# Folded expert operands on their way through DRAM: a head's 128 rows in one run, a batch's tile gathered by four loads of 32 rows

## Chip, core and metric

One core of a Trainium2 chip runs the whole program. The metric is device time in microseconds for one execution, as the median of several runs. Beside it stands one profiled execution with its trace; all rows in this document come from such a trace.

## What is computed

Three stages follow each other: an attention through 32 packed queries per head, a mixture of four experts on all tokens, and a last two-layer network.

```python
def _attn_ref(q, k, v, p):              # q, k, v: (4, 8, 576, 64), p: (4, 8, 32, 64)
    p_packed = sm_attn(p, k, v)
    return sm_attn(q, p_packed, p_packed)

def _moe_ref(x, domain_probs, w1, w2):  # x: (2304, 512), w1: (4, 512, 1024), w2: (4, 1024, 512)
    p = domain_probs / (domain_probs.sum(-1, keepdims=True) + 1e-09)
    for e in range(E):
        h = np.maximum(x @ w1[e], 0.0)
        out += p[:, e:e + 1] * (h @ w2[e])

def _moe2_ref(x, w_in, w_out, s, b):    # w_in: (512, 2048), w_out: (2048, 512)
    r = np.maximum(x @ w_in, 0.0)
    return (s * (r * r) + b) @ w_out
```

The attention's second product ends in `p_packed` and `x @ w1[e]` begins with it, so the kernel folds the two: it multiplies `p_packed` of a batch into `w1[e]` once, and the expert's first layer then reads the attention's second softmax directly. The folded operand of one expert and one batch is 256 rows (8 heads of 32 packed queries) by 1024 columns, held as two float32r parts whose sum is the float32 value.

## The kernel before

**Steps of the expert stage.** `ua` lists 256 steps: 4 experts, 4 batches, 2 halves of 288 tokens, 8 blocks of 128 hidden columns. In step i the program first runs the side work entered for that step in the table `weave` (`run`), then the first layer `m1` (line 681, 6 matmuls) of step i + 2, then the second layer `m2` (line 709, 12 matmuls) of step i. One expert and batch is 16 steps. ScalarE and VectorE split each hidden tile into two parts (lines 691 and 692) between the two. All engines work through their instructions in order, so what ScalarE or VectorE waits for in side work delays the hidden tiles behind it, and with them TensorE.

**Folded operands of experts 2 and 3.** `fold_heads` (line 478, 6 matmuls) multiplies packed heads into one piece of `w1`: for expert e, column half n, group gi of four heads, head x of a pair and z, it makes 128 rows (4 batches of 32 rows) by 512 columns. ScalarE writes the first part (line 484), VectorE the second (line 485), both into a tile `w1o` of 512 KB. There are eight folds for an expert, two `w1o` tiles each. `store_heads` (line 493) writes each tile to `w1p_dram` two steps later in the program: 16 stores an expert, 32 in all, issued by SP. `load_w1p` (line 503) reads from there what one batch needs: a tile `w1p` of 128 partitions by 1024 numbers (512 KB) for each of n = 0, 1 and gi = 0, 1, so 4 tiles a batch and 32 in all. A row of such a tile is one piece of 4 KB in DRAM. For odd batches the two heads x are swapped, as the other operand is.

**Slots.** `w1o` tiles, raw pieces of `w1` (`load_w1b`, split at line 468) and raw pieces of the last network's weights (`last_weights`, lines 570 and 575) share seven slots `q0` to `q6` of SBUF. `take` hands out the slot given back longest ago; a `w1o` slot is given back when its store is issued, so the next writer of that slot waits until the store has read it.

**Places in the table.** For expert 2 the folds of n = 0 stand in steps 105, 107, 109 and 111, those of n = 1 in 114, 116, 118 and 120; for expert 3 in 153 to 159 and 178 to 184. A store stands two steps behind its fold. The loads of an expert's batch 0 stand in the batch before it, in steps 6, 7, 13 and 14 of its 16; those of batches 1 to 3 in steps 0, 1, 2, 3 of the batch before, 14 or more steps ahead of use. Between expert 1's and expert 2's last batch, and so between 2 and 3, SP also loads the eight pieces of `w2` (line 539), each three steps ahead of its split, and all through the expert stage the weights of the last network go through a conversion: a raw load, four free steps later the first VectorE work on it (line 582), and a store (line 605).

**SP's queue.** All of these transfers but a few of ScalarE's are issued by SP in program order, an instruction each. Eight semaphores (`DMAHW0` to `DMAHW7`) take turns, so an issue also waits for the transfer eight places before it.

Of the kernel before, what the change touches and what calls it, by code (L numbers as in the profile page):

```python
# [8 lines left out]
F32 = mybir.dt.float32  # L9
# [10 lines left out]
def attention_experts_mlp_kernel(  # L20
# [26 lines left out]
    B, H, S, D = q.shape  # L47
# [4 lines left out]
    P = 128  # L52
    G = 2
# [17 lines left out]
    dram = ctx.enter_context(tc.tile_pool(name="dram", bufs=1, space=DRAM))  # L71
# [9 lines left out]
    def f32(ap):  # L81
        return ap.bitcast(F32)
# [276 lines left out]
    def give(tag):  # L359
        free4.append(tag)  # L360
# [35 lines left out]
    def w1p_tile(e, bi, c):  # L396
# [8 lines left out]

    HF = F // 2
    w1p_dram = {
        e: dram.tile([2, B, 64, 2, G, 2 * HF], F32, name=f"w1p_dram{e}")
        for e in range(2, E)
    }  # L410

# [78 lines left out]
    def store_heads(e, n, gi, x):  # L490
        for z in range(2):
            q, t = w1o.pop((e, n, gi, x, z))
            nc.sync.dma_start(  # L493
                out=w1p_dram[e][x, :, 32 * z : 32 * z + 32, n, gi],
                in_=f32(t).rearrange("a x f -> a (x f)"),
            )
            give(q)

    def load_w1p(e, bi, n, gi):
        pool = wodd if bi % 2 else keep  # L500
        t = pool.tile([P, 2, HF], F32R, tag="w1p", bufs=4, name=f"w1p_{e}{bi}{n}{gi}")
        for half in range(2):
            nc.sync.dma_start(
                out=f32(t[64 * half : 64 * half + 64]).rearrange("a x f -> a (x f)"),
                in_=w1p_dram[e][half ^ bi % 2, bi // 2 * 2 + half, :, n, gi],
            )
        w1p[e, bi, n, gi] = t

# [380 lines left out]
    with tc.manual_schedule():  # L889
# [3 lines left out]
        for gi in range(G):  # L893
# [4 lines left out]
            out=dp.rearrange("a j e -> a (j e)"),  # L898
            in_=probs.rearrange("(a j) e -> a (j e)", a=P),
# [161 lines left out]
        for e in range(E):  # L1061
            for bi in range(B):
# [12 lines left out]
                for c in range(4):  # L1075
                    n, gi = divmod(c, 2)
                    if ne > 1:
                        d = c if nb else (6, 7, 13, 14)[c]
                        at(s0 + d, load_w1p, ne, nb, n, gi)
                    if bi != B - 1 or ne < 2:  # L1080
                        continue
                    for x in range(2):
                        k = 2 * c + x
                        if n:
                            d = s0 + 2 * k - 7
                        elif ne == 2:
                            d = s0 - SB + 8 + 2 * k
                        else:
                            d = s0 - 2 * SB + NF + 2 * k
                        if x == 0:  # L1090
                            at(d - 4, load_w1b, ne, n, gi)
                        at(d, split_w1b, ne, n, gi, x)
                        at(d + 1, fold_heads, ne, n, gi, x)
                        at(d + 3, store_heads, ne, n, gi, x)
# [158 lines left out]
```

## Time and profile before

| | |
|---|---|
| median of 3 runs | 1201.96 us (1201.61 to 1205.5) |
| profiled execution | 1199.96 us, of which the span of the trace is 1198.2 us |
| TensorE matmul busy | 1122.3 us (94%) |
| VectorE, ScalarE, GpSimd busy | 683.7, 397.5, 288.5 us |
| DMA | 175.06 MB, 146 GB/s on average |
| mean granted TensorE clock | 0.970 of full speed |

TensorE is busy nearly all the time, so what is to be read is where it is not, and where it runs at a lower clock. The DMA share is the mean busy share of the core's 16 DMA engines; divided into the GB/s of the same stretch it tells how fast a busy engine moves data.

### The profile page before, as it was taken

What the parts mean: (1) busy time and instruction counts of PE and PEld (TensorE: products, weight loads), DVE (VectorE), ACT (ScalarE), POOL (GpSimd) and SP (SyncE); (2) the same over time, 40 slices, a digit from 0 to 9 for tenths busy, and PEclk for the clock granted to TensorE, in tenths of its full rate; (3) what the DMA queues carried; (4) which work ended last, traced back from release to release, by engine and by line L of the source; (5) the groups of instructions that cost most, each with busy time, mean ns of one, the idle gap of its engine ahead of it and who ended that gap; (6) DMA issues with size and microseconds to landing.
All of it is one profiled execution on the core that took longest, in us unless ns stands there. A gap on an engine that the chain in (4) does not pass through costs nothing.

```text
span 1198.2 us, 18356 instructions
## 1 busy us (share of the span) xinstructions
PE 1122.3 (94%) x7147; PEld 1047.0 (87%) x7147; DVE 683.7 (57%) x1257; ACT 397.5 (33%) x780; POOL 288.5 (24%) x345
## 2 busy tenths in 40 slices
PE   7999999999997769997976999999999999999998
PEld 5889999999996669987866999998999999999996
DVE  7866664576562315643531664357984576576654
ACT  4422223543441213331322332234563242233221
POOL 1430202233321114311313434335420111011000
PEclk9999999999998889998897999999999999999999
DMA  8624220133043446636334664133675655655532
GB/s 258 163 88 110 59 74 26 36 107 112 31 140 129 148 147 162 193 119 201 123 132 152 176 178 125 51 149 139 243 291 192 210 190 198 218 184 195 185 132 79
DMA packets 67590, 175.06 MB, mean 146 GB/s; under 512 B 10032, under 2 KB 26672, under 8 KB 67504
## 3 DMA queue, kind: packets, MB, share of 16 engines
q1 hardware_dynamic: 66656, 172.79, 44.8%
q8 instruction: 56, 0.92, 0.3%
q10 hardware_dynamic: 848, 1.11, 0.3%
q14 instruction: 30, 0.25, 0.1%
HBM read 127.44 MB, written 46.44 MB: 145 GB/s over the span
## 4 chain that ended last, share of the span: by engine, by line
PE 76%; DMA 14%; DVE 5%; issue 1%; SPq 1%; POOL 1%; ACT 1%; DVEq 0%; POOLq 0%; ACTq 0%
PE acc L709 27%; PE o L867 16%; PE h L833 14%; PE h L681 14%; DMA w1p_dram<-w1o 6%; DMA w2r<-in_moe_w_dram 4%; DMA wi11raw<-in_moe_w_in_dram 1%; DMA w1p<-w1p_dram 1%; PE s L289 1%; PE pw L379 1%; SPq L493 1%; PE pp L522 1%; DVE kT L152 1%; PE s L181 1%; PE pv L235 1%
## 5 line engine op out<-in xcount | busy, mean ns | idle before, releaser
L709 PE MATMUL acc<-hh,w2l 128*128 128x288 f32 x1024 | 310.0, 303 | 11.5 <-DVE y L724 10.8
L709 PE MATMUL acc<-hh,w2h 128*128 128x288 f32 x1024 | 309.5, 302 | 0.0
L709 PE MATMUL acc<-hl,w2h 128*128 128x288 f32 x1024 | 309.3, 302 | 0.0
L681 PE MATMUL h<-a,w1p 128*128 128x288 f32 x1536 | 262.0, 308 | 36.2 <-DVE hl L692 34.1
L681 PEld LDWEIGHTS h<-a,w1p 128*128 128x128 f32 x1536 | 226.0, 195 | 50.0 <-DVE hl L692 36.1
L692 DVE SCALAR_TENSOR_TENSOR hl<-h,hh 128x288 fp32r<-128x288 f32 x256 | 116.0, 453 | 213.7 <-ACT hh L691 212.2
L867 PE MATMUL o<-wo,gg 128*128 128x512 f32 x864 | 223.7, 393 | 3.5 <-DVE gg L801 1.9
L709 PEld LDWEIGHTS acc<-hh,w2l 128*128 128x128 f32 x1024 | 199.4, 195 | 12.6 <-ACT w1h L468 6.6
L833 PE MATMUL h<-xs,wop 128*128 128x384 f32 x1008 | 204.3, 339 | 0.7 <-DVE y L724 0.7
L709 PEld LDWEIGHTS acc<-hh,w2h 128*128 128x128 f32 x1024 | 199.7, 195 | 0.0
L709 PEld LDWEIGHTS acc<-hl,w2h 128*128 128x128 f32 x1024 | 199.5, 195 | 0.0
L833 PEld LDWEIGHTS h<-xs,wop 128*128 128x128 f32 x1008 | 181.0, 189 | 13.8 <-DVE y L724 1.4
L867 PEld LDWEIGHTS o<-wo,gg 128*128 128x128 f32 x864 | 160.8, 188 | 27.7 <-DVE gg L801 2.3
L691 ACT ACTIVATE hh<-h 128x288 fp32r<-128x288 f32 x256 | 104.2, 408 | 215.0 <-PE h L681 214.0
L735 POOL TENSOR_TENSOR x<-x,y 128x288 f32<-128x288 f32 (+2 forms) x144 | 88.1, 648 | 206.2 <-DVE y L724 206.2
L853 DVE TENSOR_TENSOR yy<-h,uv 128x384 f32<-128x384 f32 x96 | 51.0, 551 | 47.6 <-PE h L833 47.5
L787 ACT ACTIVATE yy<-yy 128x768 f32<-128x768 f32 x48 | 40.3, 839 | 113.3 <-DVE yy L853 113.3
L485 DVE TENSOR_TENSOR w1o<-pp,w1o 128x512 fp32r<-128x512 f32 x32 | 21.4, 688 | 82.4 <-ACT w1o L484 82.4
L547 POOL TENSOR_TENSOR w2l<-w2r,w2h 128x512 fp32r<-128x512 f32 x32 | 41.5, 1307 | 111.2 <-ACT w2h L546 109.6
L797 ACT ACTIVATE gg<-yy,b_sb 128x768 fp32r<-128x768 f32 x48 | 44.8, 934 | 37.3 <-DVE yy L790 36.0
L801 DVE SCALAR_TENSOR_TENSOR gg<-yy,b_sb,gg 128x768 fp32r<-128x768 f32 x48 | 55.4, 1155 | 1.6 <-ACT gg L797 1.6
L790 DVE SCALAR_TENSOR_TENSOR yy<-yy,s_sb 128x768 f32<-128x768 f32 x48 | 51.2, 1066 | 0.0
(370 smaller groups left out, 1027.4 us busy)
## 6 DMA issues: line engine op xcount, KB each, us to landing
xs<-xs_dram SPq DMA_DIRECT2D x63, 768.0 KB, 4.8
w1p_dram<-w1o SPq DMA_DIRECT2D x32, 512.0 KB
w1p<-w1p_dram SPq DMA_DIRECT2D x64, 256.0 KB, 7.7
xs_dram<-xs SPq DMA_DIRECT2D x21, 768.0 KB, 3.8
w2r<-in_moe_w_dram SPq DMA_DIRECT2D x32, 256.0 KB, 8.5
w1r<-in_moe_w_dram SPq DMA_DIRECT2D x12, 512.0 KB, 6.9
pb<-pn_dram SPq DMA_DIRECT2D x16, 288.0 KB, 13.6
out_dram<-o_sb SPq DMA_DIRECT2D x17, 256.0 KB, 2.0
```

Source lines behind the costliest of these rows:

```text
L547: nc.gpsimd.tensor_tensor(out=lo, in0=raw, in1=f32(hi), op=ALU.subtract)
L681: nc.tensor.matmul(t[:, :HT], lhsT=w1p_block(e, bi, f, gi, w), rhs=a2[bi][:, x, gi, tok], start=(n == 0), stop=(n == 3 * G - 1),)
L691: nc.scalar.activation(xh, t[:, :HT], AF.Relu)
L692: nc.vector.scalar_tensor_tensor(out=xl, in0=t[:, :HT], scalar=0.0, in1=f32(xh), op0=ALU.max, op1=ALU.subtract)
L709: nc.tensor.matmul(acc[m][:, :HT], lhsT=w[:, col], rhs=x, start=(f == 0 and n == 0), stop=(f == NF - 1 and n == 2),)
L735: nc.gpsimd.tensor_tensor(out=dst, in0=dst, in1=y[:, a - t0 : z - t0], op=ALU.add)
L790: nc.vector.scalar_tensor_tensor(out=y, in0=y, scalar=s_sb, in1=y, op0=ALU.mult, op1=ALU.mult)
L797: nc.scalar.activation(t[:, 0], y, AF.Identity, bias=b_sb)
L801: nc.vector.scalar_tensor_tensor(out=t[:, 1], in0=y, scalar=b_sb, in1=f32(t[:, 0]), op0=ALU.add, op1=ALU.subtract)
L833: nc.tensor.matmul(ps, lhsT=w[:, a, col], rhs=x[:, z, m, :], start=(n == 0), stop=(n == 3 * HK - 1),)
L853: nc.vector.tensor_tensor(out=dst, in0=ps, in1=src, op=ALU.add)
L867: nc.tensor.matmul(o_acc[i], lhsT=lhsT, rhs=w, start=(f == 0 and n == 0), stop=(f == FG - 1 and n == 2),)
```

## The change

The DRAM buffer gets another order of its dimensions, and the loads follow. Before, it is indexed [x, batch, row of 64, n, gi, column], and the 64 rows of a batch hold head z = 0 and then z = 1. A store of 128 rows therefore goes to 4 runs of 32 rows, the runs 64 rows apart. After, it is indexed [x, z, row of 128, n, gi, column]: a store's 128 rows lie one behind the other (each still a piece of 4 KB, 16 KB from the next), and a tile is gathered by 4 loads of 32 rows in place of 2 loads of 64 rows. Bytes, matmuls and vector work are the same.

```diff
     w1p_dram = {
-        e: dram.tile([2, B, 64, 2, G, 2 * HF], F32, name=f"w1p_dram{e}")
+        e: dram.tile([2, 2, P, 2, G, 2 * HF], F32, name=f"w1p_dram{e}")
...
             nc.sync.dma_start(
-                out=w1p_dram[e][x, :, 32 * z : 32 * z + 32, n, gi],
+                out=w1p_dram[e][x, z, :, n, gi],
                 in_=f32(t).rearrange("a x f -> a (x f)"),
...
-        for half in range(2):
+        for p in range(4):
+            half, z = divmod(p, 2)
+            r = 32 * (bi // 2 * 2 + half)
             nc.sync.dma_start(
-                out=f32(t[64 * half : 64 * half + 64]).rearrange("a x f -> a (x f)"),
-                in_=w1p_dram[e][half ^ bi % 2, bi // 2 * 2 + half, :, n, gi],
+                out=f32(t[32 * p : 32 * p + 32]).rearrange("a x f -> a (x f)"),
+                in_=w1p_dram[e][half ^ bi % 2, z, r : r + 32, n, gi],
             )
```

SP's instructions in the second half of expert 2's folds: stores, the first tiles of batch 0, the first pieces of `w2` (`w2r`). In the names, `w1o_21000` is expert 2, n = 1, gi = 0, x = 0, z = 0; `w1p_2000` is expert 2, batch 0, n = 0, gi = 0. Before:

```order
L493 DMA w1p_dram2_88<-w1o_21000_4515 4x32x1024
L493 DMA w1p_dram2_88<-w1o_21001_4518 4x32x1024
L503 DMA w1p_2000_4635<-w1p_dram2_88 64x1024 x2
L493 DMA w1p_dram2_88<-w1o_21010_4579 4x32x1024
L493 DMA w1p_dram2_88<-w1o_21011_4582 4x32x1024
L539 DMA w2r_20_4654<-in_moe_w2_dram 128x512
L503 DMA w1p_2001_4679<-w1p_dram2_88 64x1024 x2
```

And after:

```order
L493 DMA w1p_dram2_88<-w1o_21000_4515 128x1024
L493 DMA w1p_dram2_88<-w1o_21001_4518 128x1024
L505 DMA w1p_2000_4635<-w1p_dram2_88 32x1024 x4
L493 DMA w1p_dram2_88<-w1o_21010_4579 128x1024
L493 DMA w1p_dram2_88<-w1o_21011_4582 128x1024
L541 DMA w2r_20_4656<-in_moe_w2_dram 128x512
L505 DMA w1p_2001_4681<-w1p_dram2_88 32x1024 x4
```

The order stays; a store is one run of 128 rows where it was 4 runs of 32, and each tile takes four issues where it took two.

SP's instructions where expert 2's last batch is fetched while expert 3's first stores go out, with a raw weight piece (`wi11raw`) among them. Before:

```order
L493 DMA w1p_dram3_89<-w1o_30101_5901 4x32x1024
L503 DMA w1p_2300_6003<-w1p_dram2_88 64x1024 x2
L503 DMA w1p_2301_6033<-w1p_dram2_88 64x1024 x2
L493 DMA w1p_dram3_89<-w1o_30110_5962 4x32x1024
L493 DMA w1p_dram3_89<-w1o_30111_5965 4x32x1024
L503 DMA w1p_2310_6066<-w1p_dram2_88 64x1024 x2
L605 DMA wi_dram4_94<-wi9a_6038 128x512
L570 DMA wi11raw_6072<-in_moe2_w_in_dram 128x4x256
L503 DMA w1p_2311_6097<-w1p_dram2_88 64x1024 x2
```

And after:

```order
L493 DMA w1p_dram3_89<-w1o_30101_5925 128x1024
L505 DMA w1p_2300_6027<-w1p_dram2_88 32x1024 x4
L505 DMA w1p_2301_6059<-w1p_dram2_88 32x1024 x4
L493 DMA w1p_dram3_89<-w1o_30110_5986 128x1024
L493 DMA w1p_dram3_89<-w1o_30111_5989 128x1024
L505 DMA w1p_2310_6094<-w1p_dram2_88 32x1024 x4
L607 DMA wi_dram4_94<-wi9a_6066 128x512
L572 DMA wi11raw_6102<-in_moe2_w_in_dram 128x4x256
L505 DMA w1p_2311_6127<-w1p_dram2_88 32x1024 x4
```

Six more issues stand ahead of `wi11raw` in this stretch; nothing else has moved.

## Rows read from the trace of the kernel before

**Rows 1.** The page, part 1: busy time, share of the span, instructions.

```profile
PE 1122.3 (94%) x7147; PEld 1047.0 (87%) x7147; DVE 683.7 (57%) x1257; ACT 397.5 (33%) x780; POOL 288.5 (24%) x345
```

**Rows 2.** Stretches, m1 (L681) alone: length, busy (xmatmuls), granted clock, DMA share, GB/s.

```profile
363.30:454.70 91.40, 23.09 (x108) 19.66 (x109) 0.81 0.40 142
529.80:550.80 21.00, 4.89 (x24) 4.29 (x25) 0.76 0.41 143
562.80:576.80 14.00, 2.77 (x12) 2.42 (x13) 0.76 0.31 107
613.60:659.30 45.70, 11.47 (x54) 9.85 (x55) 0.81 0.47 159
659.30:731.10 71.80, 28.72 (x180) 25.47 (x181) 1.00 0.59 161
596.00:613.60 17.60, 6.05 (x36) 5.01 (x37) 1.00 0.25 77
```

**Rows 3.** The same stretches, folds (L478) alone; no fold in the two left out.

```profile
363.30:454.70 91.40, 6.36 (x30) 2.83 (x30) 0.81 0.40 142
529.80:550.80 21.00, 1.24 (x6) 0.48 (x6) 0.76 0.41 143
...
613.60:659.30 45.70, 1.23 (x6) 0.48 (x6) 0.81 0.47 159
...
596.00:613.60 17.60, 2.91 (x18) 1.45 (x18) 1.00 0.25 77
```

**Rows 4.** The longest of these stretches, all engines: PE, PEld, DVE, ACT, POOL busy.

```profile
363.30:454.70 91.40, 63.05 (x356) 57.93 (x355) 22.05 (x46) 18.93 (x42) 17.10 (x24) 0.81 0.40 142
```

**Rows 5.** Who waited for whom, ScalarE, whole span: total us, times, longest.

```profile
ACT w1o L484 <- DMA w1p_dram<-w1o: 70.7, 15, 9.6
ACT w2h L546 <- DMA w2r<-in_moe_w_dram: 45.9, 8, 10.8
```

**Rows 6.** Chain of waits, 340 to 460 and 510 to 670: start us, us, what.

```profile
by line: DMA w1p_dram<-w1o 33.9%; DMA w2r<-in_moe_w_dram 25.9%; PE acc L709 12.0%; PE h L681 6.7%; SPq L493 5.5%; SPq L539 2.8%; SPq L503 2.8%; issue 2.7%; DVE w1o L485 1.7%; DVE hl L692 1.7%; PE pp L478 1.5%; ACT w1o L484 1.5%; ACT hh L691
356.98 20.17 DMA w1p_dram<-w1o
412.88 13.54 DMA w2r<-in_moe_w_dram
538.84 15.05 DMA w1p<-w1p_dram
553.90 15.52 DMA wi11raw<-in_moe_w_in_dram
```

**Rows 7.** Stretches ruled by one kind of transfer, all engines; last: clock, DMA share, GB/s.

```profile
379.50:384.00 4.50, 3.98 (x17) 4.01 (x18) 2.52 (x7) 0.00 (x0) 4.04 (x8) 0.50 0.25 101
526.00:534.00 8.00, 6.43 (x49) 5.63 (x47) 1.56 (x3) 2.09 (x5) 0.00 (x0) 1.00 0.27 108
700.50:704.00 3.50, 3.50 (x29) 3.50 (x28) 2.25 (x5) 1.28 (x3) 2.82 (x4) 1.00 1.03 235
864.70:866.70 2.00, 2.00 (x12) 1.80 (x11) 2.00 (x2) 0.00 (x0) 2.00 (x2) 1.00 0.95 393
102.00:104.00 2.00, 2.00 (x26) 1.66 (x22) 0.71 (x3) 0.00 (x0) 0.00 (x0) 1.00 0.91 240
```

**Rows 8.** Instructions of tiles and lines: ns min/median/max, first and last start; landing us.

```profile
L503 SPq DMA_DIRECT2D w1p<-w1p_dram x64: 444/587/4942, 395.7 to 738.2; - x64
L493 SPq DMA_DIRECT2D w1p_dram<-w1o x32: 503/563/4167, 351.8 to 632.2; - x32
L484 ACT ACTIVATE w1o<-pp x32: 592/597/600, 349.1 to 628.2; 128x512 fp32r<-128x512 f32 x32
L485 DVE TENSOR_TENSOR w1o<-pp,w1o x32: 679/691/693, 349.7 to 628.9; 128x512 fp32r<-128x512 f32 x32
wi_dram<-wi14a SPq DMA_DIRECT2D x1, 256.0 KB, 2.1
...
DMA to landing us min/median/max: 5.4/7.7/17.2
```

## The prediction

> **What bounds the kernel now.** I read the page first: TensorE's matmuls are busy for 94% of the span [rows 1], so only stretches where TensorE is not fed can give time back. The 40 slices of the page show them around 350 to 460, 530 to 580 and 610 to 660 us. Next I asked for the busy time of such stretches with m1 alone, because its matmuls count the steps of the expert stage: six are one step [rows 2]. The stretch from 659.3 to 731.1 has 180 matmuls, 30 steps, at full granted clock: 71.80 / 30 = 2.393 us a step, undisturbed. A fold adds its six matmuls [rows 3]: from 596.0 to 613.6 there are 6 steps and 3 folds, (17.60 - 6 x 2.393) / 3 = 1.08 us each. With these two prices every disturbed stretch can be billed [rows 2, 3]:
>
> - 363.3 to 454.7 (turn to expert 2): 18 steps and 5 folds should take 43.1 + 5.4 = 48.5; it took 91.4. Lost: 42.9 us.
> - 529.8 to 550.8 (expert 3's first folds): 4 steps, 1 fold, 10.7; took 21.0. Lost: 10.3 us.
> - 562.8 to 576.8: 2 steps, 4.8; took 14.0. Lost: 9.2 us.
> - 613.6 to 659.3 (turn to expert 3): 9 steps, 1 fold, 22.6; took 45.7. Lost: 23.1 us.
>
> Together 85.5 us, 7.1% of the time. Part of a loss is plain idleness, 91.40 - 63.05 = 28.4 us in the first stretch [rows 4]. The rest is clock: there it averages 0.81, and from 379.5 to 384.0, right after a long wait, TensorE runs at 0.50, the lower of its two levels (1.2 and 2.4 GHz), while the undisturbed stretches have 1.00 [rows 2, 7]. A wait that goes takes its slow matmuls with it, and the bill in steps holds both.
>
> What ends these waits? ScalarE's waits name it: the first part of w1o waits 70.7 us for earlier stores to leave their slots, and the split of w2 waits 45.9 us for its loads [rows 5]. The chain of waits agrees: between 340 and 460 a third of it is stores, one link of 20.17 us, and a quarter is w2r, one link of 13.54 us [rows 6]. From 538.84 it goes over a w1p load of 15.05 us to a raw weight piece of 15.52 us [rows 6]. All of these sit in SP's queue among the stores.
>
> **Why the stores are slow.** From 526.0 to 534.0 stores are all that moves: 108 GB/s with a DMA share of 0.27, about a quarter of the 16 engines, although stores queue up [rows 7]. 379.5 to 384.0 reads the same, 101 at 0.25. A busy engine is fast (108 / 0.27 = 400 GB/s if all 16 were so); there are just four of them, as the store has four runs. So a store of 524 KB takes 524 / 104 = 5.0 us, 32 of them 161 us, and whatever has a share on those four engines queues behind them: w2r, w1p and wi11raw.
>
> **The change part by part.** *Stores.* With 128 rows in one run I expect 16 engines. The nearest row is the store of xs, also 128 rows from SBUF to DRAM: 393 GB/s at a share of 0.95 [rows 7]. Then a store takes 524 / 393 = 1.33 us. Against that, xs is contiguous in DRAM and this buffer has 4 KB pieces 16 KB apart; the reads of those same pieces reach 235 GB/s [rows 7], which would make it 2.23 us. I take 1.33, because 101 to 108 GB/s at a quarter share already shows writes of these pieces at the full pace of an engine, and keep 2.23 for the range.
>
> The Trainium skill, DMA: Bandwidth & Descriptors, "Latency and other measured facts", speaks against it: row pitches that are large powers of two slow a copy, 207 GB/s at its smallest pitch of 512 KiB. By that figure a store would take an estimated 2.5 us; no run here shows whether it reaches down to 16 KiB.
>
> Is that fast enough for the slots? The tightest turn is a store whose slot is written again in the next fold, 2 x 2.393 + 1.08 = 5.87 us later. After a fold the first part takes 0.60 and the second 0.69 us, the issue 0.56 [rows 8], the store 1.33, and its tail about 1.5: the 256 KB store of wi14a lands after 2.1 us [rows 8], of which 262 / 393 = 0.67 is data. That is 4.7 us; the second write of the next fold comes at 5.87 + 0.60 = 6.5. It fits by 1.8 us, and a w1 piece (524 KB, 1.3 us) ahead of it would eat most of that. At 2.23 us it would be late by a few tenths.
>
> *Loads.* Two issues of 64 rows become four of 32. Bytes are equal: the question is the rate and SP's time. SP: 64 issues more at a median of 0.587 us [rows 8] is 37.6 us in all, or 4.7 a batch. A tile then costs SP 4 x 0.587 = 2.35 us, and the table asks for one tile a step of 2.39, so SP just keeps up. What hides it is the distance: tiles of batches 1 to 3 are asked for 14 or more steps (33 us) ahead, and in batch 0 the n = 1 tiles 4 steps or more (9.6 us), against 2.35 + 2.2 + 1.5 = 6.1. If that cover went, the chain shows the price: L503 on SP is 2.8% of the 120 us from 340 to 460, 3.4 us for its issues [rows 6]; doubling adds 3.4 a turn.
>
> Rate: a 64-row load already runs at only 235 GB/s with all engines busy (share 1.03), and so does the 64-row load of k, 240 at 0.91, though k is contiguous in DRAM [rows 7]. The limit then hangs on the 64 partitions and not on the 16 KB pitch. Whether 32 partitions halve it again, no row shows. Bounds: 235 GB/s (2.2 us a tile, as now) or half, 118 (4.5 us). I take 235, the row of the same tile and the same DRAM pieces, and price the other end as a rival.
>
> The Trainium skill, SBUF — State Buffer, "Door 1: The DMA port swizzle", has it that partitions 0 to 31 reach as many ports as 0 to 63, half of all. By that rule the 32-row load keeps the 235 GB/s; the 64-row rate here agrees with its half, the 32-row one nothing here shows.
>
> *What is late next.* Per fold interval of 5.87 us in the second half there are then two stores (2.7), at most two tiles (4.5) and two w2 pieces (262 / 393 = 0.67 each): 8.5 us in the fullest interval and 4 in the next, so a backlog of 2.7 us that is gone an interval later. w2 has three steps, 7.2 us, and lands in 2.7 + 0.7 + 1.5 = 4.9. I see no stall that stays, and set 1 us for each of the four stretches: 4 us.
>
> **Sum.** The profiled execution took 1199.96 us: 1199.96 - 85.5 + 4 = 1118.5. It lies 2.0 us under the median, so I expect a median of 1120.5 us. Its own range runs from no residue and a little less (1113) to late turns at half of the folds (1127).
>
> **Rivals.**
>
> *The stores speed up by half only.* If DRAM holds them near 207 to 235 GB/s, a pair takes 4.5 to 5 us of each 5.87 and the DMA has no room for tiles and w2 beside it: the fullest interval then has 4.5 + 4.5 + 1.3 = 10.3 us, backlog 4.4, w2 late by about a microsecond at a time, and every turn of a slot by half to one. About 14 us over the two turns and 4 at the first folds: 1138. For it: the pitch. Against: the pace of a busy engine in the stores of now.
>
> *32-row loads run at half the rate.* A batch's four tiles take 18 us where the table gives them 9.6, so 8.3 us of backlog; a raw weight piece behind it lands after 8.3 + 1.3 + 1.5 = 11 us, and has four steps, 9.6. With what else is queued, 2 to 3 us a batch at five batch starts, and 4 at each turn: 20 us, 1141. Against it: the table leaves much time elsewhere.
>
> *Slower.* The stores stay at 104 GB/s, because four engines' worth is what DRAM takes at this pitch, and the second load pair lies on the chain: 3.4 us at each turn and about 2 at expert 3's first folds, 1202 + 9 = 1211. It decides as soon as a store needs 5 us as now. For it: stores have never been seen faster here. Against: the DMA share of a quarter, which says that twelve engines have nothing to do rather than that all are slow.
>
> *It does not do what it says:* the store is still cut into four runs and the loads hide: 1202.
>
> **How the numbers follow.** Forecast 0.73, stores by half 0.12, loads at half rate 0.10, slower 0.03, no change 0.02. The forecast's range with that of the first rival (0.85 in all) is 1113 to 1140. A measurement here can tell 0.3%, 3.6 us, from no change: faster 0.95, same 0.02, slower 0.03.
>
> **What would show it.** A DMA share near 1 where stores alone move, at about 400 GB/s; the store's wait on ScalarE down from 70.7 us to a few; steps of 2.4 us and 1.00 of the clock right through 363 to 455 and on; the w1p loads twice as many, at about 235 GB/s. I am wrong if stores fill the DMA at 200 GB/s, if stretches of loads alone read near 118, or if SP's issues hold w2 back.

## The result

The changed kernel takes 1115.63 us (median; 1113.75 to 1117.71), the kernel before 1202.11 beside it: a ratio of 0.9275, 95% interval 0.9251 to 0.930. The difference of the medians is 86.5 us. The profiled execution of the changed kernel took 1117.71 us, its span is 1115.9. The diff adds two lines, so lines behind it stand 2 higher in the changed kernel: m1 is L683, the split of w2 L548, the load of w1p L505; the store stays L493.

The page, parts 1, 4 (the chain's share by engine) and 6 (DMA issues: count, KB each, median us to landing):

```profile
PE 1097.7 (98%) x7147; PEld 1025.2 (92%) x7147; DVE 685.2 (61%) x1257; ACT 398.9 (36%) x780; POOL 288.9 (26%) x345
...
PE 91%; DVE 4%; POOL 1%; issue 1%; DMA 1%; ACT 1%; DVEq 0%; POOLq 0%; ACTq 0%
...
w1p_dram<-w1o SPq DMA_DIRECT2D x32, 512.0 KB, 3.8
w2r<-in_moe_w_dram SPq DMA_DIRECT2D x32, 256.0 KB, 4.1
...
w1p<-w1p_dram SPq DMA_DIRECT2D x128, 128.0 KB, 4.5
```

TensorE is busy 98% of the span where it was 94% [rows 1], and DMA is 1% of the chain of the whole span.

The same stretches as in [rows 2], from the same matmul to the same matmul, m1 (L683) alone: start and end, length, busy of PE and PEld (x instructions), granted clock, DMA share, GB/s:

```profile
366.60:415.10 48.50, 17.73 (x108) 15.11 (x109) 1.00 0.73 231
490.20:500.80 10.60, 3.92 (x24) 3.39 (x24) 1.00 1.01 320
512.90:517.60 4.70, 1.92 (x12) 1.63 (x13) 1.00 0.24 92
554.00:577.00 23.00, 8.73 (x54) 7.66 (x55) 1.00 0.74 231
577.00:648.80 71.80, 28.70 (x180) 25.46 (x181) 1.00 0.56 160
```

The last one is the undisturbed stretch, 71.80 us for 30 steps as before: the price of a step has not moved. The first four hold 33 steps and 7 folds, 33 x 2.393 + 7 x 1.08 = 86.5 us at the undisturbed prices, and take 86.80. What is lost there is 0.3 us where it was 85.5. The granted clock reads 1.00 in each, where it was 0.76 to 0.81 [rows 2].

Who waited for whom on ScalarE, whole span (total us, times, longest), and the chain of waits from 340 to 460 by line:

```profile
ACT w1o L484 <- PE pp L478: 33.1, 16, 2.1
...
ACT w2h L548 <- PE acc L711: 17.8, 15, 1.2
...
by line: PE acc L711 62.0%; PE h L683 32.2%; PE pp L478 6.0%
```

In [rows 5] the same two lines of ScalarE waited for DMAs, 70.7 and 45.9 us. They now wait for TensorE, which is the bound (one wait of 2.3 us for w2r is left); on the chain of the turn, a third stores and a quarter w2r before [rows 6], there is TensorE alone.

Stretches ruled by one kind of transfer, all engines (last three numbers: clock, DMA share, GB/s). The first has stores alone, the second loads of w1p in 32 rows alone:

```profile
359.50:362.50 3.00, 3.00 (x25) 3.00 (x24) 2.06 (x5) 1.17 (x3) 0.00 (x0) 1.00 1.03 418
415.00:424.00 9.00, 9.00 (x70) 9.00 (x69) 5.46 (x13) 3.73 (x7) 5.84 (x6) 1.00 1.05 230
```

Stores fill all 16 engines at 418 GB/s, four times the 101 to 108 of [rows 7] at four times the share. A store of 524 KB now takes 524 / 418 = 1.25 us.

One thing in these numbers needs a word. The profiled executions differ by 1199.96 - 1117.71 = 82.3 us, less than the 85.2 that the stretches gave back. The missing 2.9 us lie ahead of the change and in other work: the s matmuls at the start ran slower in this execution, by 7.4 + 6.0 - 6.2 - 4.4 = 2.8 us. Groups of TensorE's instructions from 0 to 40 us (count, busy us, mean ns, idle before; three records of the 24 are missing from one), the kernel before first, the changed one second:

```profile
L181 PE MATMUL s<-kT,pbd 128*128 128x288 f32 x24 | 6.2, 409 | 0.7 <-ACT pbd L163 0.7
...
L289 PE MATMUL s<-qT,sbd 128*128 128x288 f32 x16 | 4.4, 417 | 1.4 <-DVE sbd L272 1.4
```

```profile
L181 PE MATMUL s<-kT,pbd 128*128 128x288 f32 x21 | 7.4, 512 | 0.5 <-ACT pbd L163 0.5
L289 PE MATMUL s<-qT,sbd 128*128 128x288 f32 x16 | 6.0, 533 | 2.1 <-DVE sbd L272 2.1
```

These run some 300 us ahead of the first store, so the change cannot have slowed them. Of the kernels below, split_stores has 409 and 417 ns there, load128 411 and 537: it changes from one profiled execution to the next. Of the medians' 86.5 us, 85.2 are the stretches.

### The profile page after: what moved, and what is told of

Read it like the earlier page. It is cut to its first block, busy times and chain, and to the rows that moved or that the text cites. A ratio compares the mean times of both kernels' runs of the same rounds, so it can differ in the third digit from the quotient of the medians.

```text
span 1115.9 us, 18453 instructions
## 1 busy us (share of the span) xinstructions
PE 1097.7 (98%) x7147; PEld 1025.2 (92%) x7147; DVE 685.2 (61%) x1257; ACT 398.9 (36%) x780; POOL 288.9 (26%) x345
## 4 chain that ended last, share of the span: by engine, by line
PE 91%; DVE 4%; POOL 1%; issue 1%; DMA 1%; ACT 1%; DVEq 0%; POOLq 0%; ACTq 0%
PE acc L711 35%; PE h L683 18%; PE o L869 17%; PE h L835 15%; PE s L289 1%; PE pp L478 1%; PE s L181 1%; PE pw L379 1%; PE pp L524 1%; PE pv L235 1%; DMA k<-in_k_dram 1%; DVE gg L803 0%; POOL w2l L549 0%; POOL x L737 0%; DVE qT L152 0%
## 5 line engine op out<-in xcount | busy, mean ns | idle before, releaser
L711 PE MATMUL acc<-hl,w2h 128*128 128x288 f32 x1024 | 303.2, 296 | 0.0
L711 PE MATMUL acc<-hh,w2l 128*128 128x288 f32 x1024 | 302.5, 295 | 0.2 <-POOL w2l L549 0.2
L711 PE MATMUL acc<-hh,w2h 128*128 128x288 f32 x1024 | 302.6, 296 | 0.0
L683 PE MATMUL h<-a,w1p 128*128 128x288 f32 x1536 | 252.0, 299 | 2.1 <-DVE hl L694 0.9
L683 PEld LDWEIGHTS h<-a,w1p 128*128 128x128 f32 x1536 | 217.5, 188 | 14.4 <-issue 9.0
L711 PEld LDWEIGHTS acc<-hh,w2l 128*128 128x128 f32 x1024 | 192.3, 188 | 0.6 <-POOL w2l L549 0.4
L711 PEld LDWEIGHTS acc<-hl,w2h 128*128 128x128 f32 x1024 | 192.9, 188 | 0.0
L711 PEld LDWEIGHTS acc<-hh,w2h 128*128 128x128 f32 x1024 | 192.7, 188 | 0.0
L660 POOL TENSOR_TENSOR wo<-wo 128x512 fp32r<-128x512 f32 x16 | 23.9, 1502 | 103.7 <-ACT wo L659 103.7
```

What stands on the lines that cost most here:

```text
L683: nc.tensor.matmul(t[:, :HT], lhsT=w1p_block(e, bi, f, gi, w), rhs=a2[bi][:, x, gi, tok], start=(n == 0), stop=(n == 3 * G - 1),)
L711: nc.tensor.matmul(acc[m][:, :HT], lhsT=w[:, col], rhs=x, start=(f == 0 and n == 0), stop=(f == NF - 1 and n == 2),)
```

## The experiments

All of them compute the whole output. Ratios are to the kernel before, run beside each. "Lost" is what three spans of the expert stage (turn to expert 2, steps 111 to 136; expert 3's first folds, 160 to 176; turn to expert 3, 184 to 200) took beyond steps at 2.393 and folds at 1.085 us, counted between the same first-layer matmuls in each kernel: 43.1 + 19.7 + 23.1 = 85.9 us in the kernel before, 0.3 in the changed one.

The theory was: a store went over four engines because its DRAM side had four runs, whatever shared those engines waited behind it, and 16 engines end that. Its rivals: that the order of rows in DRAM matters; that it is the queue; that the loads' shape matters more than the store's.

**four_runs.** The changed kernel, with one row of padding behind each run of 32, so that the store has four runs again. Order of heads, loads and everything else stay.

```
-    e: dram.tile([2, 2, P, 2, G, 2 * HF], F32, ...)
+    e: dram.tile([2, 2, B, 33, 2, G, 2 * HF], F32, ...)
...
-    out=w1p_dram[e][x, z, :, n, gi],
+    out=w1p_dram[e][x, z, :, :32, n, gi],
...
-    r = 32 * (bi // 2 * 2 + half)
+    r = bi // 2 * 2 + half
...
-    in_=w1p_dram[e][half ^ bi % 2, z, r : r + 32, n, gi],
+    in_=w1p_dram[e][half ^ bi % 2, z, r, :32, n, gi],
```

> Of the change only the loads are kept: the buffer gets one spare row after every 32, so that a store again goes to four runs of 32 rows, while a tile is gathered by four loads of 32 rows as in the changed kernel. Theory (a store in four runs uses four of the 16 DMA engines, and that was the whole loss): stores at 101 to 108 GB/s and a DMA share near 0.25, ScalarE's wait for stores back at about 70 us, 1200 to 1211 us. Rival (what helped is the shorter loads or the order in DRAM): 1116 to 1130 us.

Measured: 1208.68 us (1204.76 to 1210.26), ratio 1.0068 (1.0044 to 1.0092). The whole gain is gone. A stretch of stores alone (clock, DMA share, GB/s last), and ScalarE's waits:

```profile
526.00:534.00 8.00, 8.00 (x60) 7.43 (x60) 2.93 (x6) 1.83 (x4) 0.00 (x0) 1.00 0.26 101
```

```profile
ACT w1o L484 <- DMA w1p_dram<-w1o: 72.2, 16, 9.6
ACT w2h L548 <- DMA w2r<-in_moe_w_dram: 46.1, 6, 12.7
```

Share, rate and both waits are those of the kernel before [rows 5, 7]. The loads are here the 32-row ones, and the store four-run: lost are 93.9 us, 8.0 more than before. This kernel is the prediction's slower rival made real (1211 there), and its time comes near, but the path is another one. The rival had SP's doubled load issues on the chain, where they were 2.8% from 340 to 460 [rows 6]; here they are 1.3% of it, and the stores' links rose from 33.9% to 43.1%. What grew on SP is waiting. SP's waits of the w1p loads for stores, whole span, the kernel before first, four_runs second:

```profile
SPq L503 <- DMA w1p_dram<-w1o: 0.8, 1, 0.8
```

```profile
SPq L505 <- DMA w1p_dram<-w1o: 24.8, 9, 5.7
```

With four issues a tile, a load more often takes over the semaphore of a store eight issues back and waits until that slow store has landed: 17 of the 24.8 us are such waits. How much of the 8.0 us comes of them is not shown.

**split_stores.** The other direction: the kernel before with its buffer and its 64-row loads, each store cut into four DMAs of 32 rows, one run each.

```
-    nc.sync.dma_start(out=w1p_dram[e][x, :, 32*z : 32*z + 32, n, gi], in_=f32(t)...)
+    for j in range(B):
+        nc.sync.dma_start(out=w1p_dram[e][x, j, 32*z : 32*z + 32, n, gi],
+                          in_=f32(t[32*j : 32*j + 32])...)
```

> The buffer and the 64-row loads of the kernel before; only each store is cut into four stores of 32 rows, one for each run. Nothing lies together in DRAM that did not before. Theory (the number of DMA engines that a store uses): each piece of 32 rows spreads over 16 engines, stores at over 200 GB/s, 1114 to 1122 us, with 96 more issues hidden. Rival (128 rows in one run are needed, or DRAM takes no more at this pitch): 1180 to 1205 us.

Measured: 1116.05 us (1113.62 to 1118.07), ratio 0.930 (0.9277 to 0.9323): the changed kernel's time, with the data lying in DRAM as before. What counts is over how many engines a store is spread, not that the rows lie one behind the other. Stores alone:

```profile
358.00:362.00 4.00, 4.00 (x30) 3.42 (x29) 1.07 (x3) 1.65 (x4) 0.00 (x0) 1.00 0.95 239
```

All engines are busy, at 239 GB/s (but for a dozen small packets, these are stores alone): near the 230 of the loads, which also touch 32 partitions. A pair of stores at this pace takes 4.4 us of each fold interval of 5.87, and it still cost nothing.

**act_ring.** The kernel before, its stores issued by ScalarE instead of SP, which was to free w2r and w1p from a queue with them.

```
-    nc.sync.dma_start(
+    nc.scalar.dma_start(
         out=w1p_dram[e][x, :, 32 * z : 32 * z + 32, n, gi],
```

> The kernel before with one edit: the stores are issued by ScalarE instead of SP, so that they queue in a ring of their own on the DMA engines and hold up nothing on SP. Still four runs, so 104 GB/s. Theory (the loss has two parts: slots of w1o held by slow stores, and loads queued behind stores on the same four engines): the second part, about 79 us of the chain's DMA links against 76 for the first, mostly goes: 1145 to 1175 us. Rival a (slots are all): 1195 to 1202 us. Rival b (the queue behind the stores is all): 1116 to 1125 us.

Measured: 1190.51 us (1186.77 to 1192.02), ratio 0.9917 (0.9889 to 0.9944). The expected 1145 to 1175 was missed. It came from the chain of the kernel before, where w2r held a quarter of the turn [rows 6]: I had taken that share as what would go. ScalarE's waits, the chain from 340 to 460 by line, and what the w1p loads on SP waited for stores:

```profile
ACT w1o L484 <- DMA w1p_dram<-w1o: 79.2, 17, 8.9
...
ACT w2h L546 <- DMA w2r<-in_moe_w_dram: 26.9, 10, 6.5
...
by line: DMA w1p_dram<-w1o 67.3%; PE acc L709 13.5%; PE h L681 8.6%; DMA w1p<-w1p_dram 2.9%; PE pp L478 2.9%; ACT hh L691 1.1%; issue 1.0%; ACTq L493 0.9%; ACT w1o L484 0.6%; ACT w1h L468 0.4%; DVE hl L692 0.4%; ACT w2h L546 0.4%; ACTq L484
...
SPq L503 <- DMA w1p_dram<-w1o: 28.0, 4, 12.2
```

The wait for w2r fell by 19.0 us, the wait for stores rose by 8.5, and on the chain the stores went from 33.9% to 67.3%. A wait taken off one link came back on another: as long as stores go over four engines, their pace sets the turn. The separation was not clean, though: the loads of w1p read what the stores wrote, so on SP they still waited for stores issued by ScalarE, 28.0 us where it was 0.8, and w2r stands behind them in SP's order. What w2r would gain in a queue that is wholly free of stores is not shown. The Trainium skill, DMA: Bandwidth & Descriptors, "Issuing engines are not separate DMA queues", says the queues of different issuing engines feed the same DMA engines. The trace agrees as far as it goes: where stores from ScalarE move alone, from 360 to 368, they read 106 GB/s at a share of 0.26, as they did from SP, and the gain is 9.7 us where 16 engines gave 86.5.

**two_runs, seven_engines.** If it is the count of engines, other counts must give other losses. First the changed kernel with padding after each 64 rows (two runs), then with each store cut into 119 and 9 rows. The Trainium skill, DMA: Bandwidth & Descriptors, "Why a DMA increments its semaphore by 16 and not by 1", has the engines of a DMA as the largest number up to 16 that divides the slowest dimension of both sides: 7 for 119.

```
+    e: dram.tile([2, 2, 2, 65, 2, G, 2 * HF], F32, ...)       # two_runs
+    out=w1p_dram[e][x, z, :, :64, n, gi],
+    in_=w1p_dram[e][half ^ bi % 2, z, bi // 2, 32 * half : 32 * half + 32, n, gi],
...
+    for r in (slice(0, 119), slice(119, P)):                  # seven_engines
+        nc.sync.dma_start(out=w1p_dram[e][x, z, r, n, gi], in_=f32(t[r])...)
```

> The changed kernel's loads of 32 rows, but a spare row after 64, so that a store goes to two runs of 64 rows. Theory (a store uses as many DMA engines as it has runs, and the stores' own pace sets the loss): two engines, 52 GB/s, DMA share 0.13 where stores move alone, 10 us a store; an expert's 16 stores take 161 us where four runs took 81, so about 80 us more per expert than with four runs (1208.7): about 1370 us, 1330 to 1410. Rival (the number of runs does not set the engines; four was a property of the old addresses): near 1116 or 1209 us.

> The changed kernel with each store of 128 rows cut into one of 119 rows and one of 9; 119 = 7 x 17, so that the first should use 7 DMA engines, and the second 9, one row each. Loads stay as in the changed kernel, four of 32 rows, so that SP has little more to issue. Engines 0 to 6 then have 18 rows of 0.159 us a store, 16 x 2.86 = 45.8 us for an expert's stores. Theory (the busiest engine's work against the time of the turn): in the changed kernel the stretch from 349.5 to 396.5 has a DMA share of 0.69, 32.4 us for each engine, of which stores are 16 x 1.27 = 20.3 and the rest 12.1; with 45.8 in place of 20.3 an engine has 57.9 us of work in 47, 11 us too much per expert: about 1138 us, 1128 to 1148. By the same sum four engines lose 46 us per expert (85 to 93 measured for two) and two engines 126 (240 measured). Rival a (a fold's two stores, 5.7 us, fit between two folds of 5.9): 1114 to 1122. Rival b (the 41 us that eight runs cost over its comparison were the stores' own and not SP's 256 loads): 1157 or more.

Measured: two_runs 1355.84 us (two executions, 1355.24 and 1356.43), ratio 1.1301 (1.1275 to 1.1327); seven_engines 1147.3 us (1145.79 to 1150.65), ratio 0.9568 (0.9546 to 0.9591). Stores alone in each:

```profile
360.00:380.00 20.00, 9.09 (x67) 8.28 (x65) 3.03 (x7) 2.58 (x7) 0.00 (x0) 0.86 0.13 53
```

```profile
360.00:366.00 6.00, 6.00 (x47) 5.38 (x44) 2.71 (x5) 2.40 (x5) 0.00 (x0) 1.00 0.46 182
```

The shares are 2 and 7 sixteenths (0.125, 0.44), and 2, 4, 7 and 16 engines give 53, 101, 182 and 418 GB/s, some 26 a piece: the trace agrees with the rule.

From this an estimate can be made that the prediction did not have: the work of the busiest engine. In the changed kernel the turn to expert 2 takes 47.0 us (all engines, clock, DMA share and GB/s last):

```profile
349.50:396.50 47.00, 47.00 (x337) 42.40 (x337) 25.37 (x49) 17.76 (x39) 10.44 (x17) 1.00 0.69 234
```

At a share of 0.69 each of the 16 engines works 32.4 us there; its 16 stores are 16 x 1.25 = 20.0 of it, all else 12.4. On k engines the stores come to 20.0 x 16 / k on each of these, and what goes over 47.0 is late, once for each of two experts (the kernel before lost 43.1 us for expert 2 and 42.8 for expert 3). The row of 8 is eight_runs, below, whose loads are of 16 rows:

| engines | work of the busiest | over 47.0, twice | lost, measured |
|---|---|---|---|
| 16 | 20.0 + 12.4 = 32.4 | 0 | 0.3 |
| 8 | 40.0 + 12.4 = 52.4 | 11 | 40.3 |
| 7 | 45.7 + 12.4 = 58.1 | 22 | 31.9 |
| 4 | 80.0 + 12.4 = 92.4 | 91 | 85.9 (before), 93.9 (four_runs) |
| 2 | 160 + 12.4 = 172.4 | 251 | 237.9 |

The sum holds to within 6% on two and four engines. Near the edge it is 10 us short for seven engines and 29 short for eight, so it tells that time will be lost there but not how much. It puts the edge at 16 x 20.0 / (47.0 - 12.4) = 9.2 engines; no run has between 8 and 16, so that edge is not tested.

**load128.** The mirror of the change: keep the cut on the store's side (four DMAs of 32 rows into the batches' tiles) and load a tile in one DMA of 128 rows.

```
-    e: dram.tile([2, B, 64, 2, G, 2 * HF], F32, ...)
+    e: dram.tile([B, P, 2, G, 2 * HF], F32, ...)
...
+    for j in range(B):
+        half = j % 2
+        r = 64 * half + 32 * z
+        nc.sync.dma_start(out=w1p_dram[e][j // 2 * 2 + (half ^ x), r : r + 32, n, gi],
+                          in_=f32(t[32*j : 32*j + 32])...)
...
+    nc.sync.dma_start(out=f32(t)..., in_=w1p_dram[e][bi, :, n, gi])
```

> The mirrored order: the buffer holds each batch's tile as 128 rows one behind the other, each store is cut into four of 32 rows, and a tile is one load of 128 rows. Still pieces of 4 KB, 16 KB apart. Settles what limits the loads of 64 rows to 235 GB/s. Theory (the number of partitions that a load writes): stretches of loads alone read about 390 GB/s at a share near 1. Rival (the 16 KB pitch of the reads in DRAM): about 235 GB/s still. The time by both 1113 to 1119 us, as nothing waits for loads any more.

Measured: 1114.27 us (1114.05 to 1116.35), ratio 0.9291 (0.9276 to 0.9307): the changed kernel's time within the intervals. 128-row loads alone, the last of them first and then the whole stretch, which holds some of w2r's bytes too:

```profile
416.50:418.50 2.00, 2.00 (x17) 2.00 (x17) 0.94 (x3) 0.99 (x3) 1.67 (x2) 1.00 1.02 416
411.00:418.50 7.50, 7.50 (x59) 7.50 (x58) 4.08 (x10) 3.24 (x7) 5.92 (x7) 1.00 0.99 363
```

363 to 416 GB/s come from the same 4 KB pieces 16 KB apart that 64-row loads read at 235 [rows 7]. So the loads' limit of 235 hangs on the partitions that one DMA touches and not on the pitch in DRAM. Three shapes of store and load come to 1114 to 1116 us: in these spans 0.3 us is left to lose, and TensorE is the bound.

**loads16, loads_half_columns.** Is the load's rate or its issue the next limit? Both start from the changed kernel and make eight loads a tile: one of 16 rows each, one of 32 rows and half the columns.

```
+    for p in range(8):                                        # loads16
+        half, z, y = p // 4, p // 2 % 2, p % 2
+        r = 32 * (bi // 2 * 2 + half) + 16 * y
+        nc.sync.dma_start(out=f32(t[16*p : 16*p + 16])..., in_=w1p_dram[...][..., r : r + 16, n, gi])
...
+    for y in range(2):                                        # loads_half_columns
+        nc.sync.dma_start(out=f32(t[32*p : 32*p + 32, y]),
+                          in_=w1p_dram[...][..., r : r + 32, n, gi, HF*y : HF*y + HF])
```

> The changed kernel with each tile gathered by eight loads of 16 rows instead of four of 32. Tests how much slack the load side has. If 16 partitions halve the rate of a load (about 118 GB/s where 32 and 64 give 235), a batch's four tiles keep the DMA busy for 18 us where the table gives them 9.6. Theory (tiles are asked for early enough, and SP has the time for 128 more issues at 0.42 us): 1114 to 1122 us. Rival (the price given for loads at half the rate: raw weight pieces late at batch starts, w2 late at the turns): about 1137 us, 1128 to 1150.

> The changed kernel with each load of 32 rows cut into two by columns: 256 loads of 32 rows by 512 numbers, as many issues as with loads of 16 rows, but on 32 partitions. Tells why the loads of 16 rows cost 23 us. Theory (SP's issues: 8 x 0.42 = 3.35 us a tile where the table gives a step of 2.39, so raw weight pieces come late behind 16 or more of them): again 1134 to 1144 us. Rival (16 partitions are slow, 32 are not): 1114 to 1120 us.

Measured: loads16 1138.9 us (1136.06 to 1140.15), ratio 0.9488 (0.9468 to 0.9508); loads_half_columns 1139.87 (1137.31 to 1143.08), ratio 0.9502 (0.9476 to 0.9529). For loads16 I had expected no cost; the number came out at its rival's, loads at half the rate, but not for the rival's reason. SP's instructions (start, us, count), then a stretch in the middle of them, then the chain of waits from 425 to 445, all of loads16:

```profile
408.77 0.37 SPq L541 DMA_DIRECT2D w2r<-in_moe_w_dram  x1
409.24 19.36 SPq L505 DMA_DIRECT2D w1p<-w1p_dram  x40
...
429.11 0.43 SPq L577 DMA_DIRECT2D wo4raw<-in_moe_w_out_dram  x1
```

```profile
413.00:428.00 15.00, 15.00 (x115) 15.00 (x114) 8.12 (x18) 5.76 (x11) 6.05 (x6) 1.00 0.48 136
```

```profile
by line: PE acc L711 31.0%; DMA wo4raw<-in_moe_w_out_dram 20.4%; SPq L505 16.4%; PE h L683 15.2%; issue 8.0%; DVE y L726 2.3%; DVE wo4e L584 2.2%; ACT hh L693 2.0%; SPq L607 1.9%; DVE hl L694 0.2%; ACT wo4e L587 0.1%; DVEq L584 0.1%; DVEq L
...
429.11 4.09 DMA wo4raw<-in_moe_w_out_dram
```

The DMA engines are half idle (0.48) while SP issues 40 loads without a gap, 0.484 us each, 3.87 a tile, against a step of 2.393; the raw weight piece behind them is issued late and TensorE waits for it. loads_half_columns tells issues from rate: its loads touch 32 partitions, as the changed kernel's do, and its SP reads the same:

```profile
409.75 19.46 SPq L506 DMA_DIRECT2D w1p<-w1p_dram  x40
```

The same time for the same number of issues and another shape, with the DMA engines again half idle (a share of 0.47 from 413 to 428): SP's issues are the limit, 23 to 24 us for 128 more of them. Counted step by step, loads16's loss lies in steps 136 to 160 and 200 to 224, outside the three spans above, which lost 0.8 us.

**eight_runs.** The store on eight engines, made from loads16, since only loads of 16 rows stay inside such runs.

```
-    e: dram.tile([2, 2, P, 2, G, 2 * HF], F32, ...)
+    e: dram.tile([2, 2, 8, 17, 2, G, 2 * HF], F32, ...)
...
+    out=w1p_dram[e][x, z, :, :16, n, gi],
...
-    r = 32 * (bi // 2 * 2 + half) + 16 * y
+    r = 2 * (bi // 2 * 2 + half) + y
+    in_=w1p_dram[e][half ^ bi % 2, z, r, :16, n, gi],
```

> A spare row after 16, so that a store goes to eight runs of 16 rows; a tile then takes eight loads of 16 rows, as in the kernel that took 1138.9 us with stores of one run. That one is the comparison. Theory (eight engines, 208 GB/s, 2.5 us a store; a fold's two stores take 5.0 us and fit into the 5.9 us between two folds, so slots come free in time): 1136 to 1146 us, no wait of ScalarE for stores above 5 us. Rival (anything under 16 engines costs in proportion: half of the 85 us): about 1180 us.

Measured: 1180.47 us (1180.03 to 1182.9), ratio 0.9846 (0.9826 to 0.9866). Missed: I had reckoned that a store of 2.5 us fits its interval and so costs nothing. It came out at the rival's number; but a cost in proportion to the engines would make seven_engines lose more than this kernel, and it lost less. Stores alone, ScalarE's waits, SP where a tile's loads meet the stores, and SP's waits of the loads for stores:

```profile
358.00:366.00 8.00, 8.00 (x60) 7.43 (x59) 3.68 (x7) 2.84 (x6) 0.00 (x0) 1.00 0.51 188
```

```profile
ACT w2h L548 <- DMA w2r<-in_moe_w_dram: 41.1, 12, 11.5
ACT w1o L484 <- DMA w1p_dram<-w1o: 23.0, 9, 4.4
...
380.91 8.27 SPq L505 DMA_DIRECT2D w1p<-w1p_dram  x8
...
SPq L505 <- DMA w1p_dram<-w1o: 9.9, 7, 2.1
```

The share is eight sixteenths. By the sum above, eight engines have 52.4 us of work for 47.0, 11 us lost in all; with loads16's 23 that makes 1150, and 30 us are missing. Counted step by step they are found: the three spans lost 40.3 us (0.8 in loads16), steps 136 to 160 and 200 to 208 some 26, where loads16 lost 19. So it is the sum for the stores that falls short, by 29 us. Two things that it leaves out are seen in the trace. From 414 to 418 the granted clock is 0.50, the lower of its two levels (1.2 and 2.4 GHz), after TensorE had stood still since 410. And the eight loads from 380.91 on take 8.27 us of SP's time, of which 5.2 are issues; in most of the rest the last two wait for the two stores ahead of the tile, whose semaphores they take over. How the 29 us divide between such causes is not shown. seven_engines was made to leave SP's loads as they are in the changed kernel.

## Why the prediction was right

**The bill of 85.5 us** was right: the four stretches gave back 85.2, the medians 86.5. Counting the steps in a stretch and pricing them by an undisturbed one caught idleness and low clock together.

**Why the stores were slow** was right, and shown both ways: four runs take the whole gain back with the changed loads (four_runs), and 16 engines give it with the old ones (split_stores).

**The store's price**, 1.33 us taken from the store of xs, measured 1.25. The far end of the bounds, 2.23 us from the 64-row reads, is out: that rate belongs to 64 partitions, as load128 shows with 363 to 416 GB/s at the same pitch. The row-pitch figures of the Trainium skill, DMA: Bandwidth & Descriptors, "Latency and other measured facts", whose 2.5 us the prediction gave as an estimate, do not reach down to 16 KB here: 418 GB/s written.

**The loads' rate**, 235 GB/s kept for 32 rows: 230 at a share of 1.05. The rule of the Trainium skill, SBUF — State Buffer, "Door 1: The DMA port swizzle", that 32 partitions reach as many ports as 64, now agrees with a 32-row measurement too (230, and 239 for stores of 32 rows).

**SP's issues** were mis-sized, to the safe side. The 64-row load's 0.587 us was taken for the 32-row one, which has a median of 0.418; the store's issue fell as well, from 0.563 [rows 8] to 0.332. Instructions of the two lines in the changed kernel (ns min/median/max, first and last start):

```profile
L493 SPq DMA_DIRECT2D w1p_dram<-w1o x32: 319/332/867, 355.1 to 563.5; - x32
...
L505 SPq DMA_DIRECT2D w1p<-w1p_dram x128: 302/418/1693, 380.7 to 659.5; - x128
```

By medians, 128 x 0.418 - 64 x 0.587 = 15.9 us more on SP for the loads instead of 37.6, and 7.4 less for the stores. Summed over every issue of the two lines, SP's time even fell, from 56.6 + 39.1 us (loads, stores) to 59.8 + 11.5, because issues of up to 4.9 us among the slow stores are gone [rows 8]. Whether four issues just keep up with a step (2.35 of 2.39 us by the prediction) was thus never in question: four take 1.7 to 1.9. With eight (3.9) they did not keep up, and there the cover that the prediction named went.

**The residue** is the term that was wrong: 1 us in each of four stretches was set, 0.3 in all measured. It was a caution without a row behind it. Without it the same sum gives 1114.5 for the profiled execution and 1116.5 for the median, against 1115.63. The profiled execution's 1117.71 lies near the forecast 1118.5 by luck: 2.9 us of it are the slow start, not the residue. The look at single fold intervals had found a backlog of 2.7 us; on the turn's chain nothing waits for a transfer, and over its 47.0 us the DMA engines were busy for 32.4.

**The rivals.** Stores by half (1138): out by 418 GB/s alone; and split_stores, whose stores do run at 239 GB/s, is as fast as the changed kernel, so its price was wrong as well as its condition. Loads at half rate (1141): out by 230 GB/s. loads16 came to its number by way of SP, which shows that meeting a price proves no mechanism. Slower (1211): its condition, stores on four engines with doubled loads, was made by four_runs and gave 1208.68, again not by the path that it named: SP's load issues are 1.3% of the turn's chain there. The argument against it, that the DMA share is a quarter because twelve engines have nothing to do, was the right one. No change (1202): out by the 86.5 us.

## What to carry to other kernels

Where a stretch with a full DMA queue reads a share of k sixteenths, ask which dimension of the transfer has size k: in the runs here such a DMA went over k engines, and what shared them waited. Links of the chain do not tell what mending it is worth (act_ring: a wait taken off the chain came back as another). A sum over the stretch, the busiest engine's work against the stretch's length, does so when the work is far over it; near the edge it reads too low (11 us for 40 on eight engines), so leave room. To mend it, lay out DRAM so that the large transfer has 128 rows, or cut it into DMAs of 32 rows; both came to the same time here. The limit of cutting is SP: eight issues for a tile, at 0.4 to 0.5 us each, took longer than the step of 2.393 us that the tile has.

## What was unexpected of the hardware

- SP's time for an issue depends on the shape, by median: 0.332 us for 128x1024, 0.563 for 4x32x1024, 0.587 for a load of 64 rows, 0.418 for 32 rows and for 16. Forty loads in a row take 0.48 each.
- With 4 KB pieces at a pitch of 16 KB in DRAM, 128 partitions wrote 418 GB/s, where xs, contiguous in DRAM, was written at 393 [rows 7]. 128 partitions read 363 to 416; 32 partitions wrote 239 and read 230.
- An issue can hold SP for far longer than its median while slow stores are queued. The longest issue of a store took 10.2 us on two engines, 4.3 on four (four_runs), 3.7 on seven, 2.4 on eight and 0.9 on 16, in the order of the 9.9, 5.2, 2.9, 2.8 and 1.25 us in which one store moves. Why stays open.
